# Retention attention and two dense layers on one core: the swapped copy of q's chunk 3 is made by VectorE instead of loaded

## The chip, the core and the metric

The kernel runs on one core of a Trainium2 chip. The core has TensorE (matrix multiplication into PSUM), VectorE, ScalarE and GpSimd (elementwise work), and SyncE, whose queue issues nearly all transfers between HBM and the on-chip SBUF. The metric is the device time of one execution in microseconds.

## The reference

Three stages stand behind one another, all in float32. Sizes: 4 batches, 8 heads, 576 positions, head size 64; 2304 tokens of width 512; inner widths 2048 and 1024.

```python
scores = scale * np.matmul(q, k.transpose(0, 1, 3, 2))
gamma = 1.0 - 2.0 ** (-5.0 - np.arange(H))
Dmat = np.where(rel >= 0, gamma[:, None, None] ** rel[None], 0.0)
x = np.matmul(scores * Dmat[None], v)                  # retention attention
...
h = x @ w_in
x = (h * np.clip(h + 3.0, 0.0, 6.0) / 6.0) @ w_out     # first dense stage
...
h = x @ w_in2
solu = h * softmax(h)
out = (layernorm(solu) * g_ln) @ w_out2                # second dense stage
```

## The kernel before, in words

Only the attention stage is touched. It works on 16 pairs of heads (pair 0 to 15; two heads of 64 rows fill the 128 partitions, `HEADS[0]` the lower half, `HEADS[1]` the upper). A pair's 576 positions are cut into four chunks of 128 and a rest of 64. Inside a chunk the scores are computed directly; what comes from earlier chunks goes through a running 64x64 state per head.

Per pair four tensors are loaded by SyncE: `rk` (k transposed), `rq` (q transposed), `rv` (v), `rn` (k in natural layout); `load_pair`, lines 415 to 425. The first three pairs, the early ones, go to tiles named `raw`. Loads run three pairs ahead. Behind pair 3's loads stands the first weight transfer, `wraw` (line 119), 512 KB.

The states of chunks 2 and 3 lie with the heads swapped between the halves of the partitions, so that `state[:, 2]` must meet a q of chunk 3 whose halves are swapped too. Before the change this swapped copy comes from HBM: the host appends it to `qt` as 128 further columns, and `rq[:, S:]` holds it. For pairs 3 to 15 it is a part of one transfer (352 KB instead of 288 KB), for the early pairs it is a fifth transfer of 64 KB (line 425).

The order per pair on TensorE is fixed by hand (`attention`, `mm_a`): scores `s`, last scores `z`, then `from_states` of the pair before (accumulates into `xp`, which has one buffer), the state updates `u` of this pair, `values` of the pair before (also into `xp`), and, from pair 4 on, six matmuls `h` of the first dense stage.

VectorE follows in program order. Per pair: L501 (`st4`, from `z`), L470 (state of chunk 0 copied from `u`), four multiply-adds L476 (the other states), and in between L527, `xa`: it takes the pair before out of `xp`. In every second pair come L147 and L148, the unpacking of a weight tile `wz`, and in the others L158 (its low part; for every third weight tile GpSimd does it) and L285 (`gf`, the activation of the dense stage). ScalarE scales v (L436), takes the scores out of PSUM (`st`, L455), rounds `xa` to `xb` (L260), unpacks weights (L139 `wz`, L144 `wt`, L153 `w`) and does L284 (`r`) and L290 (`g`). GpSimd masks the scores (L456), and computes the low parts of `xb` (L261, two pieces per pair that together have 576 columns), of some weights (L158) and of `g` (L291). A line 71 is a helper for the later stages.

What sets the order off TensorE is a planner inside the framework, which places instructions that are not pinned; `keep` pins one behind the last pinned one.

Of the kernel before, what the change touches and what calls it, by code (L numbers as in the profile page):

```python
# [18 lines left out]
B, H, S, D = 4, 8, 576, 64  # L19
# [55 lines left out]
def retention_hardswish_solu_kernel(ctx, tc, kt, qt, kn, vt, w1, w2i, w2o, gln, decay, place, out):  # L75


    nc = tc.nc
    ve, se, ge, te, sy = nc.vector, nc.scalar, nc.gpsimd, nc.tensor, nc.sync
# [309 lines left out]
    raws, vs, sts, sts4, states, us, xps = {}, {}, {}, {}, {}, {}, {}  # L389
    HEADS, ALL = [slice(0, 64), slice(64, 128)], slice(0, 128)  # L390
    CHUNKS = [slice(128 * c, min(128 * c + 128, S)) for c in range(NV)]
# [5 lines left out]
    keep = tc.keep_in_program_order  # L397

    def mm_a(*args, **kw):
        keep(nc.tensor.matmul(*args, **kw))  # L400

    def load_pair(pr):

        if pr >= NPAIR:
            return
        early = pr < EARLY
        if early:
            tag = "wi" if pr < 2 else "g"
            rk, rq, rn = [p0.tile([128, n], F32, tag=tag, bufs=FA, name=f"raw{pr}_{i}")
                          for i, n in enumerate((S, S + 128, 512))]  # L410
        else:
            rk = pa.tile([128, S], F32, tag="rk", bufs=3, name=f"rk{pr}")
            rq = pa.tile([128, S + 128], F32, tag="rq", bufs=4, name=f"rq{pr}")
            rn = pa.tile([128, 512], F32, tag="rn", bufs=3, name=f"rn{pr}")
        nc.sync.dma_start(out=rk, in_=kt[pr])
        n = S if early else S + 128
        nc.sync.dma_start(out=rq[:, :n], in_=qt[pr][:, :n])
        if early:
            rv = p0.tile([128, 9, D], F32, tag="g", bufs=FA, name=f"rv{pr}")
        else:  # L420
            rv = pa.tile([128, 9, D], F32, tag="rv", bufs=3, name=f"rv{pr}")
        nc.sync.dma_start(out=rv, in_=vt[pr])
        nc.sync.dma_start(out=rn, in_=kn[pr])
        if early:
            nc.sync.dma_start(out=rq[:, n:], in_=qt[pr][:, n:])
        raws[pr] = rk, rq, rn.rearrange("p (c d) -> p c d", d=128), rv

    def prep(pr):
# [32 lines left out]
    def chunk_states(pr):  # L461

        rn, v = raws[pr][2], vs[pr]
        up = ps_a.tile([128, 4, 64], F32, tag="u", bufs=1, name=f"u{pr}")
        state = states[pr] = pa.tile([128, 4, 64], F32, tag="state", bufs=2, name=f"state{pr}")
        for c in range(4):
            for h in range(2):
                o = HEADS[1 - h if c == 3 else h]
                mm_a(up[o, c], rn[:, c, HEADS[h]], v[:, 4 * h + c], start=(c == 0), stop=(c == 3))
        ve.tensor_copy(out=state[:, 0], in_=up[:, 0])  # L470
        for c, to, at in (
            (1, ((ALL, ALL),), H + pr % NP), (2, tuple(zip(HEADS, HEADS[::-1])), H + pr % NP),
            (3, ((ALL, ALL),), H + 2 * NP + pr % NP),
        ):
            for i, o in to:
                ve.scalar_tensor_tensor(  # L476
                    out=state[o, c], in0=state[i, c - 1], scalar=decay_sb[i, at:at + 1], in1=up[i, c],
                    op0=ALU.mult, op1=ALU.add,
                )

    def places():

# [50 lines left out]
    def attention():  # L533

        for pr in range(NPAIR + 1):
            if pr < NPAIR:
                scores(pr)
                last_scores(pr)
            if pr:
                from_states(pr - 1)  # L540
            if pr < NPAIR:
                idle_mm(N_IDLE.get(pr, 0))
                if pr == 0:
                    places()
            yield pr
            if pr < NPAIR:
                load_pair(pr + EARLY)
                chunk_states(pr)
                prep(pr + 1)
                if pr < NP:  # L550
                    widen(pr)
            yield pr
            if pr:
                values(pr - 1)
            yield pr
            if pr == 1:
                tc.keep_in_program_order(nc.sync.dma_start(out=gln_sb, in_=gln))
# [16 lines left out]
    for pr in range(EARLY):  # L574
        load_pair(pr)
# [3 lines left out]
    for h in range(2):  # L579
        ge.affine_select(  # L580
            out=mask4[HEADS[h]], in_=mask4[HEADS[h]], compare_op=ALU.is_ge, fill=0.0,
# [332 lines left out]
    ve, se, ge, te, sy = (Pinned(tc, e) for e in (ve, se, ge, te, sy))  # L914
# [145 lines left out]
```

## Time and profile before

| | |
|---|---|
| median of 3 runs | 650.05 us (649.01 to 650.99) |
| profiled execution | 651.0 us, of which the span from first to last instruction is 649.3 |
| TensorE busy | 641.0 us (99%) |
| VectorE, ScalarE, GpSimd busy | 333.5 (51%), 370.0 (57%), 325.8 us (50%) |
| transfers | 114.01 MB, mean 176 GB/s |
| attention stage | about the first 84 us of the span |

The shares say how much an engine works in all, not who is waited for. Attention takes an eighth of the span, and there all engines hand work to each other pair by pair; so it is read from the engines' timelines, where the time in square brackets is the idle time before an instruction and the name behind it what ended it.

### The profile page before, as it was taken

How to read it: one execution, taken by the hardware profiler on the slowest of the kernel's cores; microseconds unless marked ns; L12 is line 12 of the kernel's file. 1: busy time of each engine (PE TensorE's matmuls, PEld its weight loads, DVE VectorE, ACT ScalarE, POOL GpSimd, SP SyncE). 2: the span in 40 equal slices, each digit the busy share in tenths (PEclk: the TensorE clock that was granted, in tenths of full speed). 3: DMA queues.
4: the chain of work that ended last, by engine and by line, in shares of the span. 5: the costliest groups of instructions: out<-in, count | busy, mean ns of one | idle time of the engine just before them, and what ended most of it. 6: DMA issues, size and time to landing. Idle time of an engine off the chain costs nothing.

```text
span 649.3 us, 11131 instructions
## 1 busy us (share of the span) xinstructions
PE 641.0 (99%) x4178; PEld 533.4 (82%) x4178; DVE 333.5 (51%) x618; ACT 370.0 (57%) x653; POOL 325.8 (50%) x342
## 2 busy tenths in 40 slices
PE   8899999999999999999999999999999999999998
PEld 5777878888889888888888888889988888888887
DVE  2767635334104454143555446112588878878750
ACT  5788846556325665164356337215277768787582
POOL 4687844223222434045044014606379899999453
PEclk9999999999999999999999999999999999999999
DMA  8999517277015161557765645239795333534442
GB/s 307 371 380 365 208 33 260 97 260 258 33 41 191 63 194 59 169 195 292 257 218 161 240 158 167 97 121 369 256 229 145 81 98 99 130 81 98 74 104 68
DMA packets 80459, 114.01 MB, mean 176 GB/s; under 512 B 42642, under 2 KB 47890, under 8 KB 80404
## 3 DMA queue, kind: packets, MB, share of 16 engines
q1 hardware_dynamic: 80256, 113.27, 55.0%
q8 instruction: 33, 0.54, 0.4%
q14 instruction: 22, 0.18, 0.1%
q10 hardware_dynamic: 148, 0.02, 0.0%
HBM read 71.85 MB, written 31.98 MB: 160 GB/s over the span
## 4 chain that ended last, share of the span: by engine, by line
PE 95%; DMA 3%; ACT 1%; issue 0%; DVE 0%; SPq 0%; ACTq 0%
PE h L272 31%; PE x L297 20%; PE o L71 15%; PE h L71 13%; PE acc L297 8%; PE xp L400 3%; PE x L71 2%; PE s L400 2%; DMA wraw<-in_w_dram 1%; PE u L400 1%; DMA raw<-in_qt_dram 1%; DMA raw<-in_kn_dram 1%; DVE w L158 0%; PE z L400 0%; ACT st L455 0%
## 5 line engine op out<-in xcount | busy, mean ns | idle before, releaser
L291 POOL TENSOR_TENSOR g<-gf,g 128x512 fp32r<-128x512 f32 (+1 forms) x78 | 96.5, 1237 | 215.2 <-ACT g L290 205.1
L297 PE MATMUL x<-g,w 128*128 128x512 f32 x576 | 132.0, 389 | 0.0
L272 PE MATMUL h<-xb,w 128*128 128x512 f32 (+1 forms) x600 | 129.8, 360 | 0.1
L297 PEld LDWEIGHTS x<-g,w 128*128 128x128 f32 x576 | 108.1, 188 | 22.5
L272 PEld LDWEIGHTS h<-xb,w 128*128 128x128 f32 x600 | 98.5, 189 | 17.9 <-issue 1.9
L285 DVE SCALAR_TENSOR_TENSOR gf<-r,h 128x512 f32<-128x512 f32 (+1 forms) x80 | 50.5, 632 | 120.1 <-ACT r L284 105.0
L71 PE MATMUL o<-w,lt 128*128 128x512 f32 (+1 forms) x456 | 103.0, 378 | 0.0
L71 PEld LDWEIGHTS o<-w,lt 128*128 128x128 f32 x456 | 82.4, 188 | 16.3 <-POOL lt L71 0.4
L284 ACT ACTIVATE r<-h,half 128x512 f32<-128x512 f32 (+1 forms) x80 | 50.6, 635 | 64.4 <-PE h L272 64.4
L272 PE MATMUL h<-xB,w 128*128 128x512 f32 x360 | 82.4, 389 | 0.0
L272 PEld LDWEIGHTS h<-xB,w 128*128 128x128 f32 x360 | 67.6, 188 | 14.0
L290 ACT ACTIVATE g<-gf 128x512 fp32r<-128x512 f32 (+1 forms) x78 | 46.1, 591 | 44.0 <-DVE gf L285 38.6
L71 POOL TENSOR_TENSOR lt<-lT,lt 128x512 fp32r<-128x512 f32 x36 | 61.0, 1713 | 13.4 <-ACT lt L71 13.4
L297 PE MATMUL acc<-g,w 128*128 128x512 f32 (+1 forms) x264 | 61.9, 361 | 0.0
L71 ACT ACTIVATE e<-h,stat 128x1024 f32<-128x1024 f32 x36 | 41.3, 1148 | 34.9 <-DVE stat L71 34.8
L297 PEld LDWEIGHTS acc<-g,w 128*128 128x128 f32 x264 | 46.9, 188 | 8.8
L147 DVE TENSOR_SCALAR wz<-wz 128x512 int32<-128x512 int32 x44 | 29.5, 671 | 47.7 <-ACT wz L139 47.6
L71 PE MATMUL h<-w2t,xt 128*128 128x512 f32 x216 | 53.5, 389 | 0.0
L71 PEld LDWEIGHTS h<-w2t,xt 128*128 128x128 f32 x216 | 40.3, 188 | 8.2
L71 PE MATMUL h<-w2b,xt 128*128 128x512 f32 x162 | 39.8, 390 | 0.0
L139 ACT ACTIVATE wz<-wraw 128x512 f32<-128x512 f32 x44 | 29.2, 663 | 17.6 <-DMA wraw<-in_w_dram 8.9
L261 POOL TENSOR_TENSOR xb<-xa,xb 128x512 fp32r<-128x512 f32 (+7 forms) x32 | 28.3, 906 | 16.8 <-ACT xb L260 16.6
(114 smaller groups left out, 842.9 us busy)
## 6 DMA issues: line engine op xcount, KB each, us to landing
wraw<-in_w_dram SPq DMA_DIRECT2D x32, 512.0 KB, 5.0
xs<-xb SPq DMA_DIRECT2D x12, 512.0 KB, 7.7
xB<-xs SPq DMA_DIRECT2D x12, 512.0 KB, 6.3
rv<-in_vt_dram SPq DMA_DIRECT2D x16, 288.0 KB, 6.3
x2l<-x2s SPq DMA_DIRECT2D x18, 256.0 KB, 4.2
x2f<-x2o SPq DMA_DIRECT2D x18, 256.0 KB, 3.6
x2r<-x2f SPq DMA_DIRECT2D x9, 512.0 KB, 4.4
rq<-in_qt_dram SPq DMA_DIRECT2D x13, 352.0 KB, 6.8
```

Of the source, the lines that this page charges most:

```text
L71: return lambda *args, **kw: self.keep(op(*args, **kw))
L139: first = se.activation(out=z.bitcast(F32), in_=raw[:, :, 1].bitcast(F32), func=ACTF.Prelu, scale=2.0 ** -112, alpha=2.0 ** 32)
L147: ve.tensor_scalar(out=z, in0=z, scalar1=3, scalar2=None, op0=ALU.logical_shift_left)
L261: ge.tensor_tensor(out=x[:, 1, c], in0=src, in1=f32(x[:, 0, c]), op=ALU.subtract)
L272: mm = nc.tensor.matmul(hp, w1t[ff, 0][:, a, c], xb[t, p][:, b, :n], start=(p == 0 and i == 0), stop=(p == NP - 1 and i == 2),)
L284: se.activation(out=r, in_=hp, func=ACTF.Relu, scale=1.0 / 6.0, bias=half)
L285: ve.scalar_tensor_tensor(out=gf, in0=r, scalar=1.0, in1=hp, op0=ALU.min, op1=ALU.mult)
L290: se.activation(out=g[ff][:, 0], in_=gf, func=ACTF.Copy)
L291: ge.tensor_tensor(out=g[ff][:, 1], in0=gf, in1=f32(g[ff][:, 0]), op=ALU.subtract)
L297: te.matmul(acc, w1t[ff, 1][:, a, c], g[:, b], start=(first and i == 0), stop=(last and i == 2))
L400: keep(nc.tensor.matmul(*args, **kw))
```

## The change

The host no longer appends the swapped chunk; `load_pair` loads the 576 columns of q for every pair, in one transfer each. In `chunk_states` VectorE copies the two halves of chunk 3 crosswise into `rq[:, S:]` (two copies of 64 partitions x 128 columns), ahead of the states. These copies, the state copy and the multiply-adds are now pinned.

```diff
--- before.py
+++ after.py
@@ -413,16 +413,13 @@
             rq = pa.tile([128, S + 128], F32, tag="rq", bufs=4, name=f"rq{pr}")
             rn = pa.tile([128, 512], F32, tag="rn", bufs=3, name=f"rn{pr}")
         nc.sync.dma_start(out=rk, in_=kt[pr])
-        n = S if early else S + 128
-        nc.sync.dma_start(out=rq[:, :n], in_=qt[pr][:, :n])
+        nc.sync.dma_start(out=rq[:, :S], in_=qt[pr])
         if early:
             rv = p0.tile([128, 9, D], F32, tag="g", bufs=FA, name=f"rv{pr}")
         else:
             rv = pa.tile([128, 9, D], F32, tag="rv", bufs=3, name=f"rv{pr}")
         nc.sync.dma_start(out=rv, in_=vt[pr])
         nc.sync.dma_start(out=rn, in_=kn[pr])
-        if early:
-            nc.sync.dma_start(out=rq[:, n:], in_=qt[pr][:, n:])
         raws[pr] = rk, rq, rn.rearrange("p (c d) -> p c d", d=128), rv
 
     def prep(pr):
@@ -467,16 +464,19 @@
             for h in range(2):
                 o = HEADS[1 - h if c == 3 else h]
                 mm_a(up[o, c], rn[:, c, HEADS[h]], v[:, 4 * h + c], start=(c == 0), stop=(c == 3))
-        ve.tensor_copy(out=state[:, 0], in_=up[:, 0])
+        rq = raws[pr][1]
+        for h in range(2):
+            keep(ve.tensor_copy(out=rq[HEADS[1 - h], S:], in_=rq[HEADS[h], CHUNKS[3]]))
+        keep(ve.tensor_copy(out=state[:, 0], in_=up[:, 0]))
         for c, to, at in (
             (1, ((ALL, ALL),), H + pr % NP), (2, tuple(zip(HEADS, HEADS[::-1])), H + pr % NP),
             (3, ((ALL, ALL),), H + 2 * NP + pr % NP),
         ):
             for i, o in to:
-                ve.scalar_tensor_tensor(
+                keep(ve.scalar_tensor_tensor(
                     out=state[o, c], in0=state[i, c - 1], scalar=decay_sb[i, at:at + 1], in1=up[i, c],
                     op0=ALU.mult, op1=ALU.add,
-                )
+                ))
 
     def places():
 
@@ -1016,7 +1016,6 @@
     kt, qt = (np.array(a.transpose(0, 2, 1).reshape(NPAIR, 2 * D, S)) for a in (k, q))
     for a in (kt, qt):
         a[:, :, 512:] = np.roll(a[:, :, 512:], D, axis=1)
-    qt = np.concatenate([qt, np.roll(qt[:, :, 384:512], D, axis=1)], axis=2)
     kn = k[:, :512].reshape(NPAIR, 2, 4, 128, D).transpose(0, 3, 2, 1, 4).reshape(NPAIR, 128, 512)
     vt = np.empty((NPAIR, 128, 9, D), np.float32)
     vt[:, :, :8] = v[:, :512].reshape(NPAIR, 2, 4, 128, D).transpose(0, 3, 1, 2, 4).reshape(NPAIR, 128, 8, D)
```

TensorE's, ScalarE's and GpSimd's instructions keep their order. VectorE's and SyncE's change in attention alone. Three places follow; the number behind a name belongs to the buffer and differs between the two kernels.

VectorE in the states of pair 4, where a weight tile's L158 stands; before:

```order
L476 SCALAR_TENSOR_TENSOR state_471<-state_471,decay_sb,u_470 128x64
L501 TENSOR_TENSOR st_535<-z_534,mask_116 128x64
L158 TENSOR_TENSOR w_0_0_507<-wz,w_0_0_507 128x512
L470 COPY state_559<-u_558 128x64
L476 SCALAR_TENSOR_TENSOR state_559<-state_559,decay_sb,u_558 128x64
L476 SCALAR_TENSOR_TENSOR state_559<-state_559,decay_sb,u_558 64x64 x2
L527 TENSOR_TENSOR xa_593<-xp_539,tab_sb_115 128x576
```

L158 stands between L501 and the state copy. The same stretch of VectorE in the changed kernel:

```order
L501 TENSOR_TENSOR st_540<-z_539,mask_116 128x64
L469 COPY rq_283<-rq_283 64x128
L158 TENSOR_TENSOR w_0_0_512<-wz,w_0_0_512 128x512
L469 COPY rq_283<-rq_283 64x128
L470 COPY state_564<-u_563 128x64
L476 SCALAR_TENSOR_TENSOR state_564<-state_564,decay_sb,u_563 128x64
L476 SCALAR_TENSOR_TENSOR state_564<-state_564,decay_sb,u_563 64x64 x2
L527 TENSOR_TENSOR xa_600<-xp_544,tab_sb_115 128x576
```

The low part of the weights, L158, was ahead of the state copy and is now between the two copies of q's halves.

VectorE around pair 13, from the weights' L147 on (`state_1433` before, `state_1456` after, is pair 13's); before:

```order
L147 TENSOR_SCALAR wz<-wz 128x512
L148 ISA wz<-wz,wt 128x1024
L501 TENSOR_TENSOR st_1417<-z_1416,mask_116 128x64
L470 COPY state_1433<-u_1432 128x64
L476 SCALAR_TENSOR_TENSOR state_1433<-state_1433,decay_sb,u_1432 128x64
L476 SCALAR_TENSOR_TENSOR state_1433<-state_1433,decay_sb,u_1432 64x64 x2
L527 TENSOR_TENSOR xa_1459<-xp_1421,tab_sb_112 128x576
```

The state copy follows L501 directly. The same stretch of VectorE in the changed kernel:

```order
L147 TENSOR_SCALAR wz<-wz 128x512
L148 ISA wz<-wz,wt 128x1024
L501 TENSOR_TENSOR st_1440<-z_1439,mask_116 128x64
L469 COPY rq_1156<-rq_1156 64x128 x2
L470 COPY state_1456<-u_1455 128x64
L476 SCALAR_TENSOR_TENSOR state_1456<-state_1456,decay_sb,u_1455 128x64
L476 SCALAR_TENSOR_TENSOR state_1456<-state_1456,decay_sb,u_1455 64x64 x2
L527 TENSOR_TENSOR xa_1484<-xp_1444,tab_sb_112 128x576
```

Two copies are added between L501 and the state copy; the rest stands as it did, with `xa` of pair 12 behind the states. The same two copies stand at this place in every pair.

SyncE's transfers of pair 2 and pair 3, up to the first weight transfer; before:

```order
L415 DMA raw_0_152<-in_kt_dram 128x576
L417 DMA raw_1_153<-in_qt_dram 128x576
L422 DMA rv_157<-in_vt_dram 128x576
L423 DMA raw_2_154<-in_kn_dram 128x512
L425 DMA raw_1_153<-in_qt_dram 128x128
L415 DMA rk_209<-in_kt_dram 128x576
L417 DMA rq_210<-in_qt_dram 128x704
L422 DMA rv_214<-in_vt_dram 128x576
L423 DMA rn_211<-in_kn_dram 128x512
L119 DMA wraw<-in_w_dram 128x1024
```

Ten transfers, of which the fifth and a part of the seventh carry the swapped chunk. The same stretch of SyncE's queue in the changed kernel:

```order
L415 DMA raw_0_150<-in_kt_dram 128x576
L416 DMA raw_1_151<-in_qt_dram 128x576
L421 DMA rv_155<-in_vt_dram 128x576
L422 DMA raw_2_152<-in_kn_dram 128x512
L415 DMA rk_206<-in_kt_dram 128x576
L416 DMA rq_207<-in_qt_dram 128x576
L421 DMA rv_211<-in_vt_dram 128x576
L422 DMA rn_208<-in_kn_dram 128x512
L119 DMA wraw<-in_w_dram 128x1024
```

The fifth transfer of the early pairs is gone and pair 3's q has 576 columns instead of 704.

## Rows read from the trace of the kernel before

**Rows 1.** DMA view, 0 to 90 us: GB/s in 40 slices of 2.25 us

```profile
GB/s 46 305 327 394 333 359 371 377 394 374 380 371 356 362 322 374 392 395 400 397 362 349 331 404 395 366 277 396 413 372 313 364 144 7 16 220 7 0 195 38
```

**Rows 2.** Stretches: us, busy us of each engine, granted clock, DMA share, GB/s

```profile
0.00:26.40 26.40, 21.72 (x420) 15.35 (x420) 10.52 (x34) 16.10 (x37) 13.97 (x35) 1.00 0.94 335
...
84.00:649.30 565.30, 562.14 (x2703) 472.78 (x2692) 283.10 (x479) 305.27 (x507) 266.51 (x251) 1.00 0.51 155
```

**Rows 3.** Chain of waits, 0 to 140 us: start us, us, what

```profile
12.80 7.50 DMA wraw<-in_w_dram
```

**Rows 4.** Timeline, TensorE: start us, us, engine, line, operation, count, [idle before]

```profile
22.76 1.48 PE L400 MATMUL s<-rq,rk 64*64 64x128 f32 x29 [1.57 <-ACT st L455]
...
24.33 0.27 PE L400 MATMUL xp<-st,v 64*64 64x64 f32 x2
...
48.59 0.22 PE L400 MATMUL xp<-st,v 64*64 64x64 f32 x2
...
79.27 4.47 PE L272 MATMUL h<-xb,w 128*128 128x512 f32 x18
```

**Rows 5.** Timeline, VectorE, 20 to 84 us

```profile
22.35 0.21 DVE L470 COPY state<-u 128x64 f32<-128x64 f32 x1
...
23.52 0.76 DVE L527 TENSOR_TENSOR xa<-xp,tab_sb 128x576 f32<-128x576 f32 x1
...
30.75 0.23 DVE L470 COPY state<-u 128x64 f32<-128x64 f32 x1 [0.19 <-PE u L400]
...
45.30 0.23 DVE L470 COPY state<-u 128x64 f32<-128x64 f32 x1
...
46.49 0.76 DVE L527 TENSOR_TENSOR xa<-xp,tab_sb 128x576 f32<-128x576 f32 x1
...
68.84 0.22 DVE L501 TENSOR_TENSOR st<-z,mask 128x64 f32<-128x64 f32 x1
69.19 0.23 DVE L470 COPY state<-u 128x64 f32<-128x64 f32 x1
...
70.37 0.76 DVE L527 TENSOR_TENSOR xa<-xp,tab_sb 128x576 f32<-128x576 f32 x1
```

**Rows 6.** Timeline, ScalarE, 38 to 84 us

```profile
48.91 0.78 ACT L260 ACTIVATE xb<-xa 128x448 fp32r<-128x448 f32 x2
...
68.09 0.77 ACT L260 ACTIVATE xb<-xa 128x384 fp32r<-128x384 f32 x2
...
71.16 0.78 ACT L260 ACTIVATE xb<-xa 128x320 fp32r<-128x320 f32 x2
```

**Rows 7.** Timeline, GpSimd, 20 to 84 us

```profile
22.16 1.54 POOL L261 TENSOR_TENSOR xb<-xa,xb 128x512 fp32r<-128x512 f32 x2 [3.52 <-ACT xb L260]
...
30.06 1.79 POOL L261 TENSOR_TENSOR xb<-xa,xb 128x512 fp32r<-128x512 f32 x2 [1.48 <-ACT xb L260]
...
44.77 1.29 POOL L158 TENSOR_TENSOR w<-wz,w 128x512 fp32r<-128x512 f32 x1
46.01 1.30 POOL L291 TENSOR_TENSOR g<-gf,g 128x512 fp32r<-128x512 f32 x1
...
68.69 1.65 POOL L261 TENSOR_TENSOR xb<-xa,xb 128x384 fp32r<-128x384 f32 x2 [1.13 <-ACT xb L260]
```

**Rows 8.** Tile wz (count: ns min/median/max), then GpSimd and VectorE from their timelines

```profile
L147 DVE TENSOR_SCALAR wz<-wz x37: 419/429/1498, 84.4 to 401.5; 128x512 int32<-128x512 int32 x37
...
96.19 1.29 POOL L291 TENSOR_TENSOR g<-gf,g 128x512 fp32r<-128x512 f32 x1 [6.61 <-ACT g L290]
...
96.70 1.06 DVE L147 TENSOR_SCALAR wz<-wz 128x512 int32<-128x512 int32 x1 [1.25 <-ACT wz L139]
...
240.86 1.65 POOL L291 TENSOR_TENSOR g<-gf,g 128x512 fp32r<-128x512 f32 x1 [4.95 <-ACT g L290]
242.47 1.75 POOL L158 TENSOR_TENSOR w<-wz,w 128x512 fp32r<-128x512 f32 x1
...
241.46 1.60 DVE L158 TENSOR_TENSOR w<-wz,w 128x512 fp32r<-128x512 f32 x1
```

## The prediction

> **What bounds the kernel now.** I read the page's shares first, then the stretches, the chain of waits, and last the timelines of the engines through attention. The granted clock is 1.00 in the stretches, so it plays no part [rows 2]. After 84 us TensorE is busy 562.14 of 565.30 us [rows 2]: what comes later there has at most 3.2 us of idle time in which to be made good, and the change touches none of it. What counts is attention, the first 84 us.
>
> Attention has two parts. Until some 26 us the transfers set the pace: TensorE is busy 21.72 of 26.40 us, and the chain runs through a weight transfer that is issued at 12.80 and takes 7.50 us, so to 20.30 [rows 2, 3]. ScalarE stands in line behind it with the states that free the score banks, and TensorE waits 1.57 us before 22.76 for them [rows 4]. From there TensorE runs pair after pair almost without a gap, some 4.8 us a pair (VectorE's state copies of pairs 5 and 13, at 30.75 and 69.19, stand 38.44 apart) [rows 5].
>
> VectorE and ScalarE look half idle in the shares, and they are not free. In pair 13 VectorE's L501 starts at 68.84 and the state copy at 69.19; three multiply-adds follow, and xa from 70.37 to 71.13; ScalarE's xb, which reads it, starts at 71.16 [rows 5, 6]. From there w, r, gf, g, st, wz, wt and xb of the other pair follow each other, and VectorE takes up L148 and L501 again. This circle takes two pairs and keeps step with TensorE, with 0.2 us to spare before the state copy (0.35 from L501's start, of which some 0.15 is L501 itself). TensorE's own slack is larger: in pair 8 xa ends at 47.25 and TensorE overwrites its bank from 48.59, 1.3 us later [rows 4, 5].
>
> **What goes: 16 pieces of 64 KB.** Ahead of the weight transfer four go (three transfers of line 425, and 64 of pair 3's 352 KB). From 2.25 to 20.25 us the slices read 305 to 394 GB/s, mean 357 [rows 1], so 65,536 bytes take 0.18 us, four 0.73. The transfer lands that much earlier, and so does TensorE's 22.76. The three issues that go from SP's queue were ahead of the same transfer and fall into this. The other twelve pieces lie in the part where TensorE never waits for a load: nothing.
>
> **What comes: 32 copies on VectorE**, two per pair, 64x128 fp32 from SBUF to SBUF, between L501 and the state copy. The rows hold no such copy. The nearest are the state copy (0.23 us, 64 elements, from PSUM) and L147 (fp32-sized, SBUF to SBUF, 512 elements: 0.42 at its shortest) [rows 5, 8]. Alone I put a copy at 0.07 (a quarter of what L147 takes below once it may run) to 0.23 us, and take 0.15, the middle.
>
> The larger question is GpSimd. L147 takes 0.419 to 1.498 us [rows 8], and the long ones are those that meet a GpSimd instruction: at 96.70 it is issued while GpSimd works from 96.19 to 97.48, and ends at 97.76, 0.28 after it. It does not run slower beside it, it waits for the end. And the two take turns: GpSimd's g, at 240.86, lasts 1.65 us and ends at 242.51; VectorE's L158, issued at 241.46, ends 0.55 later, at 243.06; the GpSimd instruction that stands behind, recorded at 242.47, takes 1.75 instead of 1.29, as it waits for VectorE in its turn.
>
> The Trainium skill (SBUF — State Buffer, section "Who interferes with whom") states it as a rule that speaks against this change: a copy in VectorE's two-port mode and a GpSimd instruction shut each other out for a whole instruction, and the one issued first goes first. By that rule the sum below holds; were a 64-partition copy outside it, the second rival would. The trace agrees for L147 (0.42 alone, 1.06 behind GpSimd); no row shows such a copy. The skill's table of VectorE costs (VectorE: DVE Perf Modes, section on the TRN2 errata) gives 58 cycles and half a cycle per element, an estimate of 0.13 us a copy; by it the sum would end some 0.3 us lower.
>
> So what does GpSimd do where the copies now stand? In the odd pairs ScalarE's xb (68.09, directly behind wt) hands the first of two L261 pieces to GpSimd at 68.69, while VectorE is in L148; L501 follows at 68.84, and a copy can be issued from about 69.0 [rows 5 to 7]. Both sides start from the same wt, so GpSimd stays ahead even when everything is late. The first copy waits for the first piece; then GpSimd's second piece, which has been waiting, goes ahead of the second copy. The state copy starts after both pieces and both copies. In pair 13 L261 ends at 70.34, the state copy stood at 69.19: 1.15 later, in pair 5 31.85 against 30.75, 1.10; these are the first and the last of five pairs (5, 7, 9, 11, 13). With two copies of 0.15 that makes 1.42 each. Nothing hides it: xa is queued behind on VectorE, xb behind xa on ScalarE, and the circle returns to VectorE that much later.
>
> **The sum.** Lateness of the circle against the trace:
> - pair 3: L261 ends at 23.70, plus 0.30 makes 24.00 against 22.35, 1.65, less the 0.73 of the start: 0.9. TensorE feels it at once: xa ends at 24.28 and TensorE's 24.33 follows it [rows 4, 5, 7].
> - pair 4: the order puts L158 between its copies; the second one waits for it and for a small piece of L261: some 0.4, the two copies and a handover.
> - pairs 5, 7, 9, 11, 13: 5 x 1.42 = 7.1.
> - pairs 8 and 14, where GpSimd also has the weights' L158 (44.77 and, behind it, g at 46.01 to 47.31): the copies wait for both, so the state copy moves from 45.30 to 47.6, 2.3 later; xa ends at 49.55. ScalarE's xb for it stood at 48.91: 0.64 more for the circle. TensorE's 48.59 waits for it too: 0.96 [rows 4 to 7].
> - pairs 6, 10, 12: GpSimd is idle there; 0.3 to 0.5 on VectorE lies under TensorE's slack of 1.3 and off the circle. Pairs 0 to 2 wait for TensorE anyway: nothing. Pair 15 lies under the h matmuls of 4.47 us from 79.27 [rows 4].
>
> Up to pair 14 the circle is late by 0.9 + 0.4 + 7.1 + 0.64 = 9.0; in pair 14 TensorE waits another 0.96, so it is late by 10.0 when attention ends, and keeps it, since it has no idle time later. The profiled run took 651.0 us (span 649.3, 1.7 around it): 661.0. It stands 0.95 above the median of 650.05, so the forecast is 660.0. With copies of 0.07 or 0.23, 14 of them in this sum, it moves by 1.1 either way; if TensorE's slack of 1.3 were kept to the end, 658.7; if the bank waits behind attention add up, 662. Own range 656.5 to 664.
>
> **Rivals.**
> - *Only the first copy waits.* The second follows before GpSimd's second piece. L261's first piece has 384 of 576 columns, some 1.1 of the 1.65 us, so pair 13 waits to 69.8: 0.6 + 0.3 = 0.9, five of them 4.5, with 0.5 from pair 3 and 0.4 from pair 4; pair 8 waits to 46.06, within the slack: 5.4, so 655.5. For it: the copies stand side by side in VectorE's queue. Against: at 241.46 the waiting GpSimd went before VectorE's next instruction. 0.17.
> - *The copies do not wait for GpSimd at all*, as the state copy does not. An odd pair then costs two copies (0.46 at most) less 0.2, so 0.3; five make 1.3, pairs 3 and 4 some 0.9, less 0.73: 1.5, of which TensorE's slack takes most: 650.5. For it: only half the partitions, other shapes than in the rows. Against: L147 and its length. 0.13.
> - *The other side: the start decides.* If copies are free and the thinner queue of loads clears not only the 0.73 but all of the wait of 1.57 before 22.76 and some of the rest of the start (26.40 less 21.72 is 4.7 us of idle time), TensorE gains 2 us: 648. It decides once VectorE is done with pair 3's states before 22.35 + 0.73. Against: GpSimd works from 22.16 to 23.70 just there. 0.06.
> - That the change is not carried out is excluded by the order of the instructions, which shows 32 copies and three transfers fewer.
>
> **Chances.** The forecast 0.64, the rivals 0.17, 0.13, 0.06. About 0.3%, 2 us, is what a measurement of this kernel can tell from no change. Slower by more: the forecast, the first rival and a little of the second, 0.82; within: most of the second and some of the third, 0.13; faster: 0.05. The range reaches down through the first rival, 652.5, and up to 665.
>
> **What would show it.** VectorE's line 469 with two classes: some 0.2 us alone (pairs 6, 10, 12) and 0.5 to 1.2 us beside GpSimd, each ending shortly after a GpSimd instruction; in the odd pairs L261's second piece between the two copies. TensorE with waits of 1 us and more per two pairs in front of xp or s, put down to xa or st, and the h matmuls of 79.27 some 10 us later. The first weight transfer 0.7 us earlier. It is wrong if the copies are short everywhere (650.5), or if the circle has slack that I do not see, such as a wait of ScalarE for TensorE that swallows the lateness; then TensorE's pairs stay some 4.8 us apart.

## The result, and the profile after

The changed kernel takes **657.83 us** (median of 4 runs, 657.39 to 658.13) against 650.06 (649.01 to 650.99): 1.0134 times as long, 95% interval 1.0122 to 1.0147. It is slower by 7.8 us; 660.0 were predicted, 656.5 to 664 as the likeliest case's own range.

Its profiled execution took 657.54 us, span 655.7. The stretches (us, busy us of each engine, granted clock, DMA share, GB/s), to be held against [rows 2]:

```profile
0.00:26.40 26.40, 23.11 (x424) 16.23 (x426) 14.70 (x46) 17.52 (x40) 15.57 (x37) 1.00 0.97 351
26.40:90.00 63.60, 58.55 (x1071) 46.32 (x1069) 50.82 (x126) 47.06 (x106) 44.06 (x55) 1.00 0.74 254
90.00:655.70 565.70, 562.02 (x2690) 472.47 (x2686) 282.70 (x480) 306.41 (x508) 267.10 (x252) 1.00 0.51 155
```

The same view of the kernel before, for the part of attention behind the start:

```profile
26.40:84.00 57.60, 57.10 (x1068) 45.26 (x1070) 39.87 (x106) 48.64 (x111) 45.30 (x58) 1.00 0.85 306
```

Behind 90 us TensorE idles 3.7 us, hardly more than the 3.2 of before. Between 26.4 and 90 us it now idles 5.1 of 63.60 us, where it idled 0.5 of 57.60. What was lost was lost in attention. VectorE's timeline there (start, us, line, operation, count, [idle before]), answering to [rows 5]:

```profile
19.97 1.34 DVE L469 COPY rq<-rq 64x128 f32<-64x128 f32 x2
...
46.24 2.04 DVE L469 COPY rq<-rq 64x128 f32<-64x128 f32 x2
48.20 0.21 DVE L470 COPY state<-u 128x64 f32<-128x64 f32 x1
...
68.48 0.46 DVE L469 COPY rq<-rq 64x128 f32<-64x128 f32 x2
...
72.81 0.22 DVE L501 TENSOR_TENSOR st<-z,mask 128x64 f32<-128x64 f32 x1
73.05 1.34 DVE L469 COPY rq<-rq 64x128 f32<-64x128 f32 x2
74.31 0.21 DVE L470 COPY state<-u 128x64 f32<-128x64 f32 x1
...
75.48 0.76 DVE L527 TENSOR_TENSOR xa<-xp,tab_sb 128x576 f32<-128x576 f32 x1
```

And GpSimd's timeline, answering to [rows 7]:

```profile
45.67 1.28 POOL L158 TENSOR_TENSOR w<-wz,w 128x512 fp32r<-128x512 f32 x1
46.91 1.29 POOL L291 TENSOR_TENSOR g<-gf,g 128x512 fp32r<-128x512 f32 x1
...
69.06 1.27 POOL L291 TENSOR_TENSOR g<-gf,g 128x512 fp32r<-128x512 f32 x1 [0.89 <-ACT g L290]
...
72.66 1.65 POOL L261 TENSOR_TENSOR xb<-xa,xb 128x384 fp32r<-128x384 f32 x2 [1.15 <-ACT xb L260]
```

The two copies of pair 12 (68.48) meet an idle GpSimd and take 0.46 us together. Those of pair 13 (73.05) meet the two pieces of L261, which end at 74.31, and the state copy starts at 74.31. One by one these four are:

```profile
73.05 0.78 DVE L469 COPY rq<-rq 64x128 f32<-64x128 f32 x1
73.85 0.54 DVE L469 COPY rq<-rq 64x128 f32<-64x128 f32 x1
72.66 1.09 POOL L261 TENSOR_TENSOR xb<-xa,xb 128x384 fp32r<-128x384 f32 x1 [1.15 <-ACT xb L260]
73.71 0.60 POOL L261 TENSOR_TENSOR xb<-xa,xb 128x192 fp32r<-128x192 f32 x1
```

The first copy ends at 73.83, 0.08 behind the first piece (73.75), and the second at 74.39, 0.08 behind the second (74.31). Those of pair 8 (46.24) meet the weight's L158 and, behind it, g, which ends at 48.20; the state copy starts at 48.20. Of the 32 copies 15 last 0.22 to 0.27 us, the others 0.41 to 1.26.

TensorE's timeline shows who waits for it:

```profile
20.28 1.94 PE L400 MATMUL s<-rq,rk 64*64 64x128 f32 x32 [0.52 <-ACT st L452]
...
50.18 0.27 PE L400 MATMUL xp<-st,v 64*64 64x64 f32 x2 [0.83 <-DVE xa L527]
...
82.88 0.27 PE L400 MATMUL xp<-st,v 64*64 64x64 f32 x2 [0.86 <-DVE xa L527]
...
94.55 2.96 PE L297 MATMUL acc<-g,w 128*128 128x512 f32 x12 [0.51 <-DVE xa L527]
```

TensorE's waits for xa in the first 95 us are, in the kernel before and then in the changed one (us in total, times, longest):

```profile
PE xp L400 <- DVE xa L527: 0.2, 1, 0.2
PE xp L400 <- DVE xa L527: 4.0, 7, 0.9
```

The first row of the timeline above starts 2.48 us earlier than its partner at 22.76, though, where 0.73 had been predicted; the first weight transfer landed at 17.74 instead of 20.30:

```profile
10.34 7.40 DMA wraw<-in_w_dram
```

This is the chain of waits, against [rows 3]. Two questions stood open: whether the turns with GpSimd are the whole price, and what the start is worth.

### The profile page after: what moved, and what is told of

It is laid out like the page before. It is cut to its first block, busy times and chain, and to the rows that moved or that the text cites. A ratio compares the mean times of both kernels' runs of the same rounds, so it can differ in the third digit from the quotient of the medians.

```text
span 655.7 us, 11157 instructions
## 1 busy us (share of the span) xinstructions
PE 643.7 (98%) x4177; PEld 535.0 (82%) x4178; DVE 348.2 (53%) x650; ACT 371.0 (57%) x653; POOL 326.7 (50%) x342
## 4 chain that ended last, share of the span: by engine, by line
PE 88%; DMA 4%; POOL 3%; DVE 2%; ACT 1%; issue 1%; SPq 0%; ACTq 0%; DVEq 0%; POOLq 0%
PE h L272 28%; PE x L297 20%; PE o L71 15%; PE h L71 13%; PE acc L297 8%; DMA wraw<-in_w_dram 3%; PE x L71 2%; POOL xb L261 1%; POOL st L453 1%; DVE xa L527 1%; PE xp L400 1%; DMA raw<-in_kt_dram 1%; ACT xb L260 1%; PE s L400 1%; PE u L400 1%
## 5 line engine op out<-in xcount | busy, mean ns | idle before, releaser
L147 DVE TENSOR_SCALAR wz<-wz 128x512 int32<-128x512 int32 x44 | 29.7, 675 | 44.4 <-ACT wz L139 44.3
L261 POOL TENSOR_TENSOR xb<-xa,xb 128x512 fp32r<-128x512 f32 (+7 forms) x32 | 29.4, 940 | 24.1 <-ACT xb L260 24.1
```

What stands on the lines that cost most here:

```text
L147: ve.tensor_scalar(out=z, in0=z, scalar1=3, scalar2=None, op0=ALU.logical_shift_left)
L261: ge.tensor_tensor(out=x[:, 1, c], in0=src, in1=f32(x[:, 0, c]), op=ALU.subtract)
```

## The experiments

All ratios are to the kernel before on the same chip, with a 95% interval. The median of the kernel before is 650.06 us in the result above and 648.72 to 649.14 in the experiments, so times of different experiments are compared through the ratios.

### The copies alone

The loads of the kernel before, and the copies on top:

```diff
+        for h in range(2):
+            keep(ve.tensor_copy(out=rq[HEADS[1 - h], S:], in_=rq[HEADS[h], CHUNKS[3]]))
```

> The loads of the kernel before and the copies of the changed one (which write the same numbers over what was loaded). It shows the price of the copies alone. Theory (copies cost some 8 to 10 us over their waits, the loads' gain is separate): the changed kernel's 657.8 and the start's 2 to 2.5 on it, 659.5 to 660.5 us. Rival (the load's gain is 0.73): 658.6 us. Second rival (what slows attention is that loads are missing, not the copies): 650 us.

Measured: 658.66 against 649.14 us, 1.0146 (1.0133 to 1.016), so 9.5 us. The copies carry the whole loss. Against 1.0134 for the changed kernel the missing loads are worth 0.8 us, with an uncertainty (some 1.2) larger than the number.

### Half as long

```diff
-keep(ve.tensor_copy(out=rq[HEADS[1 - h], S:], in_=rq[HEADS[h], CHUNKS[3]]))
+keep(ve.tensor_copy(out=rq[HEADS[1 - h], S:S + 64], in_=rq[HEADS[h], 384:448]))
```

> As the kernel with loads and copies, but each copy moves the first 64 of the 128 columns (the rest stays as loaded): 32 copies of half the length. Theory (a copy costs the end of the GpSimd instruction that it meets, whatever its length): 1.0 to 1.015 times the kernel before, close to the 1.0146 of whole copies: 1.013 (1.011 to 1.0145), and a copy that meets GpSimd idle takes some 0.15 us instead of 0.22. Rival (elements are paid for, by VectorE's own time or by the share of a port): half of the surplus, 1.007.

Measured: 1.0147 (1.0133 to 1.0161), a hair above the range expected and the same as with whole copies. The row of this tile on VectorE (count: ns min/median/max, first and last start):

```profile
L472 DVE COPY rq<-rq x26: 189/517/1258, 20.9 to 86.2; 64x64 f32<-64x64 f32 x26
```

Half the elements save 32 ns where a copy is alone (189 against 221 with whole copies) and nothing where it waits (1258 against 1257). Elements aren't what is paid for.

### Half as many

```diff
-        for h in range(2):
+        for h in range(1):
             keep(ve.tensor_copy(out=rq[HEADS[1 - h], S:], in_=rq[HEADS[h], CHUNKS[3]]))
```

> As the kernel with loads and copies, but one copy for a pair instead of two. Theory (a price for each turn with GpSimd): in odd pairs the state copy starts at the end of the first piece of the subtraction, 0.56 us earlier than with two (0.6 instead of 1.15 late), and in pairs 8 and 14, which meet 1.3 us instructions, 1.2 us earlier: 5 x 0.56 + 2 x 1.2 = 5.2 of the 9.5 us go, ratio to the kernel before 1.0066 (1.005 to 1.009). Rival (the first copy alone waits, the second rides behind it for nothing): 1.0135 or more.

Measured: 1.0084 (1.0068 to 1.0099), 5.5 us: one copy less saves 4.0 of the 9.5, somewhat less than the 5.2 worked out. The rival, that the first copy alone waits, would have left all of it. From L501's start to the state copy's, pair 8 takes 1.07 us instead of 2.21, and the odd pairs from 5 to 13 take 1.07 to 1.34 instead of 1.51 to 1.52. There is a price for each turn.

### The same place and length, another form

```diff
-            keep(ve.tensor_copy(out=rq[HEADS[1 - h], S:], in_=rq[HEADS[h], CHUNKS[3]]))
+            keep(ve.tensor_reduce(
+                out=rq[HEADS[1 - h], S:], in_=rq[HEADS[h], CHUNKS[3]].unsqueeze(2), op=ALU.add, axis=AX.X,
+            ))
```

> The copies stay ahead of the state copy, in another form of the same length: a sum over an axis of one element, 64x128 each. Theory (it is the turn with GpSimd that costs, and this form takes no turn): each lasts about 0.2 to 0.25 us beside GpSimd's subtraction, the pair's two 0.45, of which 0.2 fits into the slack of the odd pairs: six such pairs by 0.25 are 1.5 over the 648.0 of no cost, so about 649.5 us (648.5 to 651.5). Rival (VectorE's own time for two more instructions, or what their pins do to its order, is the price): 657.8 us as the changed kernel, since there are as many instructions in the same places. Second rival (this form waits for GpSimd as well): 0.5 to 0.8 us each in odd pairs, 657 to 659 us.

Measured: 650.97 us, 1.0021 (1.001 to 1.0031). That is 1.4 us over the kernel before by this ratio and 1.8 by the medians, where the changed kernel loses 7.8. VectorE around the same pair 13:

```profile
67.73 0.69 DVE L148 CUSTOM_DVE_ANT_0 wz<-wz,wt 128x1024 uint16<-128x1024 uint16 x1 [0.15 <-ACT wt L144]
68.34 0.22 DVE L503 TENSOR_TENSOR st<-z,mask 128x64 f32<-128x64 f32 x1
68.59 0.57 DVE L469 TENSOR_REDUCE rq<-rq 64x128 f32<-64x128 f32 x2
69.08 0.21 DVE L472 COPY state<-u 128x64 f32<-128x64 f32 x1
```

and GpSimd beside it, in the same kernel:

```profile
68.19 1.66 POOL L261 TENSOR_TENSOR xb<-xa,xb 128x384 fp32r<-128x384 f32 x2 [1.17 <-ACT xb L260]
```

L261 works from 68.19 to 69.85, and both sums run in the middle of it in 0.57 us. All 26 on this tile last 279 to 284 ns. As many instructions in the same places, each a little longer than a lone copy, cost about a fifth: most of the price is the wait and not VectorE's time. By the Trainium skill (SBUF — State Buffer, "Who interferes with whom") a sum over an axis never contends with GpSimd on this chip, while a copy in two-port mode does. The trace agrees on both: 0.28 us for each sum beside L261, against 0.78 and 0.54 for the two copies at the same place.

### The loads alone, and the pins alone

Without the extra loads and without copies:

```diff
-        for h in range(2):
-            keep(ve.tensor_copy(out=rq[HEADS[1 - h], S:], in_=rq[HEADS[h], CHUNKS[3]]))
...
-            (1, state[:, 0], rq[:, CHUNKS[1]]), (3, state[:, 2], rq[:, S:]),
+            (1, state[:, 0], rq[:, CHUNKS[1]]), (3, state[:, 2], rq[:, CHUNKS[3]]),
```

> Neither the extra load nor the copies; the matmuls of chunk 3 read the chunk unswapped (left out: the swap of its halves). It shows the price of the loads alone. Theory (the start won 2 to 2.5 us because the weight transfer landed at 17.7 where it had landed at 20.3): 648.0 us (647.3 to 648.8). Rival (four pieces of 64 KB are worth 0.73 us at the rate of the slices, and the rest of the earlier landing was chance of one run): 649.3 us (648.9 to 649.6).

Measured: 649.12 against 649.14 us, 1.0002 (0.9992 to 1.0012). My theory's 2 to 2.5 us fell. The rival's 649.3 was reckoned from 650.05; against this chip's 649.14 even its 0.73 isn't seen.

The kernel before with the pins, which moved no instruction on any engine:

> The kernel before with only the pins on the state copy and the multiply-adds; on every engine its instructions stand in the same order as before, so its profile is also a second look at the kernel before. Theory (pins cost nothing, and the late scores of pair 3 in the profile of before, at 22.76 us, were one execution's chance in the first loads): within 0.1 % of before, and TensorE begins pair 3's scores near 20.3 to 21.0 us. Rival (the loads of the extra chunk made that start late every time): the scores begin at 22.3 to 22.9 us again. Second rival (pins cost): over 1 us slower than before.

Measured: 1.0005 (0.9996 to 1.0013); the pins cost nothing. Its profile (span 647.6) is a second look at the kernel before. SyncE's and TensorE's timelines there:

```profile
11.43 0.33 SPq L119 DMA_DIRECT2D wraw<-in_w_dram  x1
```

```profile
21.07 1.83 PE L400 MATMUL s<-rq,rk 64*64 64x128 f32 x31 [1.50 <-ACT st L455]
...
77.59 4.47 PE L272 MATMUL h<-xb,w 128*128 128x512 f32 x18
```

The weight transfer is issued at 11.43 and takes 7.2 us, so it lands at 18.6; the scores begin at 21.07, and the 18 h matmuls 1.68 us earlier than in [rows 4]. The execution of before that I had read was a late one: by 1.4 to 1.7 us from pair 2 to its end. In the four experiments that have all the extra loads the transfer lands at 18.5 to 18.7; in the eight profiles that lack those ahead of it, the changed kernel's 17.74 among them, at 17.6 to 18.1. The middles are 0.8 apart: 0.73 was the right size.

Finally the lighter start alone: extra chunk not loaded for pairs 0 to 3, and loaded for the rest.

```diff
-        n = S if early else S + 128
+        n = S if pr <= EARLY else S + 128
...
-        if early:
-            nc.sync.dma_start(out=rq[:, n:], in_=qt[pr][:, n:])
...
+        for h in range(2 if pr <= EARLY else 0):
+            keep(ve.tensor_reduce(...))
```

> The extra piece is left out of the loads of pairs 0 to 3 alone, whose swap is done by the summing form ahead of the state copy; pairs 4 to 15 as in the kernel before. It shows what the lighter start is worth when nothing is paid for it later. Theory (the start's gain in the changed kernel's profile was chance of one execution of the kernel before; four pieces of 64 KB are worth 0 to 0.7 us and TensorE gives them back in the circle): 0.9995 (0.9985 to 1.001). Rival (2.5 us as in the profiles): 0.996 to 0.997.

Measured: 648.63 against 648.93 us, 0.9997 (0.9988 to 1.0007). The landing of the weights comes earlier, the end does not, to within 0.7 us. Where it goes isn't settled.

### Where else the copies can stand

Behind the states, where VectorE idles before L147 or L158:

```diff
-            keep(ve.tensor_copy(out=rq[HEADS[1 - h], S:], in_=rq[HEADS[h], CHUNKS[3]]))
-        keep(ve.tensor_copy(out=state[:, 0], in_=up[:, 0]))
+        ve.tensor_copy(out=state[:, 0], in_=up[:, 0])
...
+            keep(ve.tensor_copy(out=rq[HEADS[1 - h], S:], in_=rq[HEADS[h], CHUNKS[3]]))
```

> The same 32 copies in the same form, moved from ahead of the state copy to behind the last multiply-add of the pair, where VectorE idles; loads as in the changed kernel. Theory (the copies wait for GpSimd's subtractions ahead of the state copy, and this wait stretches the circle VectorE - ScalarE - GpSimd): the wait leaves the circle and the earlier start stays, so about 648.0 us (647.0 to 649.5), faster than both kernels; the copies may still last 0.2 to 0.9 us each, and it costs nothing. Rival (fewer loads or the pins are what slows attention, or the copies cost wherever they stand on VectorE): 655 to 658 us.

Measured: 651.15 us, 1.0031 (1.0019 to 1.0043), faster than the changed kernel by 1.0% and still slower than before, where the theory had it faster. TensorE in pairs 0 and 1:

```profile
10.55 0.80 PE L400 MATMUL xp<-raw,state 64*64 64x128 f32 x12 [0.46 <-DVE raw L479]
...
15.56 0.27 PE L400 MATMUL xp<-st,v 64*64 64x64 f32 x2 [0.81 <-DVE xa L527]
```

In the first pairs the copies stand ahead of what TensorE waits for. So the sums took the first four pairs, ahead of the states, and the copies the rest, behind them:

```diff
+        for h in range(2 if pr <= EARLY else 0):
+            keep(ve.tensor_reduce(...))
...
+        for h in range(2 if pr > EARLY else 0):
+            keep(ve.tensor_copy(out=rq[HEADS[1 - h], S:], in_=rq[HEADS[h], CHUNKS[3]]))
```

> No extra load; the first four pairs swap by the summing form ahead of the state copy, the others by copies behind the last multiply-add. Theory (what the copies behind the states cost was in the first pairs, where xa and the matmuls of chunk 3 stood behind them, and what the summing form cost was in the later ones): both costs go, ratio 1.000 to the kernel before (0.999 to 1.0015), as with neither load nor copy, and some 1.3 % faster than the changed kernel. Rival (every placement costs some 1.5 us, by the time that it takes from VectorE): 1.002 to 1.003.

Measured: 650.71 us, 1.0034 (1.0022 to 1.0047). The theory's 1.000 fell, and the number is just above what the rival gave. VectorE in pair 4 shows a reason other than the rival's:

```profile
27.01 0.48 DVE L483 COPY rq<-rq 64x128 f32<-64x128 f32 x2
27.52 0.43 DVE L147 TENSOR_SCALAR wz<-wz 128x512 int32<-128x512 int32 x1
28.09 1.55 DVE L148 CUSTOM_DVE_ANT_0 wz<-wz,wt 128x1024 uint16<-128x1024 uint16 x1
29.56 0.21 DVE L505 TENSOR_TENSOR st<-z,mask 128x64 f32<-128x64 f32 x1
```

with GpSimd beside it:

```profile
27.58 2.23 POOL L261 TENSOR_TENSOR xb<-xa,xb 128x512 fp32r<-128x512 f32 x2 [1.27 <-ACT xb L260]
```

The copies wait for nothing, but L147 and L148 come behind them, and L148, otherwise 0.69 us, runs into L261's two pieces (27.58 to 29.81) and lasts 1.55. In the other pairs L148 still lasts 0.69, so this is 0.86 of some 2 us; the rest isn't accounted for pair by pair. So I put nothing ahead of L147: the odd iterations, which have none, swap two pairs at once, the own by copies, the next by sums:

```diff
+        if pr >= 5 and pr % 2:
+            swap(pr, False)
+            if pr + 1 < NPAIR:
+                swap(pr + 1, True)
```

> No extra load; nothing more ahead of L147 and L148: the first five pairs swap by the summing form ahead of the state copy, and from pair 5 on the odd iterations, which have no L147, swap their own pair by copies and the next pair by the summing form behind the last multiply-add, in the 1.1 us in which VectorE waits for the weight's words. Theory (what placement behind the states cost was that the copies pushed L147 and L148 0.5 us later, into GpSimd's subtraction: L148 lasted 1.55 us instead of 0.69 in pair 4): the surplus goes, ratio 1.000 to the kernel before (0.999 to 1.0015); L148 lasts 0.69 us in all pairs. Rival (the time on VectorE, 0.45 to 0.56 us a pair, costs wherever it stands): 1.0025 to 1.004 as in the last run.

Measured: 651.35 us, 1.0034 (1.0022 to 1.0046). L148 lasts 0.69 throughout, as expected, and the surplus stays, so L148 alone was not what cost it. VectorE's copies again:

```profile
L471 DVE TENSOR_REDUCE rq<-rq x14: 279/280/282, 20.4 to 73.2; 64x128 f32<-64x128 f32 x14
L472 DVE COPY rq<-rq x12: 444/644/1203, 31.1 to 81.5; 64x128 f32<-64x128 f32 x12
...
  PE xp L400: 1.4, 3
```

The last row is who waited for them: TensorE's chunk 3, 1.4 us in three places. No copy is short any more; GpSimd selects `st` and then subtracts in just this stretch, as in pair 9 (two copies, and GpSimd beside them):

```profile
51.25 1.51 DVE L472 COPY rq<-rq 64x128 f32<-64x128 f32 x2
50.40 1.22 POOL L453 TENSOR_SCALAR_AFFINE_SELECT st<-st 128x512 f32<-128x512 f32 x2
51.67 1.56 POOL L261 TENSOR_TENSOR xb<-xa,xb 128x384 fp32r<-128x384 f32 x2
```

The last kernel changes only these copies to sums:

```diff
-            swap(pr, False)
+            swap(pr, True)
```

> As the last kernel but one, with the two halves of the own pair in the odd iterations in the summing form too: no swap takes the form of a copy any more, and all stand behind the states from pair 5 on. Theory (what was left there was again the turn with GpSimd: the copies met its selection of st and its next subtraction, lasted 0.44 to 1.20 us and held the matmuls of chunk 3 up): every swap lasts 0.28 us, 1.12 for four beside 1.1 us of idle time, and the ratio to the kernel before falls from 1.0034 to 1.000 (0.999 to 1.0015). Rival (the time on VectorE costs wherever it stands): 1.003 to 1.004 again.

Measured: **648.62 against 648.84 us, 0.9999 (0.9985 to 1.0012)**. All 26 last 279 to 282 ns, and nobody waits for them. VectorE in this kernel:

```profile
49.68 1.20 DVE L471 TENSOR_REDUCE rq<-rq 64x128 f32<-64x128 f32 x4
50.91 0.74 DVE L158 TENSOR_TENSOR w<-wz,w 128x512 fp32r<-128x512 f32 x1
```

The four sums fill the gap ahead of L158 with 1.20 us of work, and the 2 us are gone. It makes the swap without its loads at no cost, 1.3% faster than the changed kernel, and no faster than the kernel before: with neither loads nor copies there was nothing to be had.

## Why the prediction was right, and where its sizes were off

The second look at the kernel before (span 647.6) is the better measure for single steps, since its start is not late.

- **The start, 0.73.** The transfer lands some 0.8 earlier. That this is kept to the end was wrong or is too small to see: 0.0 and -0.2 us with 0.7 either way in the two runs that have it alone. The third rival (the start decides, 648) is refuted by the same two runs.
- **A copy takes 0.07 to 0.23 alone, 0.15 taken.** It takes 0.22, so the upper end. With it the sum would have grown by 1 us. The copies did not add even the 0.15: one that waits ends 0.08 behind GpSimd's instruction, whatever it takes alone, and in pair 13 the state copy starts at L261's end (74.31) and not 0.3 behind it.
- **Copies wait for GpSimd, both of them.** Right, by the rows above, and shown by the sums, which run beside L261. The first rival (only the first copy waits, 655.5) is refuted by the run with one copy. The second (no wait) describes the kernel with the sums. Its 650.5 was 0.45 above the kernel before, and the sums cost 1.4 by their ratio, so its price was too low.
- **The lateness of the circle, 9.0 up to pair 14.** VectorE's state copy of pair 15, in the second look and in the changed kernel:

```profile
76.84 0.23 DVE L470 COPY state<-u 128x64 f32<-128x64 f32 x1
86.00 0.21 DVE L470 COPY state<-u 128x64 f32<-128x64 f32 x1
```

  It is 9.16 late. That this meets 9.0 is in part luck, since the terms behind it are off both ways. Up to pair 4 the sum had 1.3, and the state copy of pair 4 is 0.46 late. From there to pair 13 it had 7.74, and 6.35 are lost. For pairs 14 and 15 it had nothing in the circle (0.96 on TensorE), and 2.35 are lost. An odd pair was put at 1.42 and an even one beside it (6, 10, 12) at nothing; from state copy to state copy the even ones lose 0.35 to 0.5 as well and the odd ones 0.5 to 0.9, so two pairs lose 1.0 to 1.3 together. The state copies of pairs 8 and 9 lose 2.0 and 0.04, where 0.64 and 1.42 stood: 2.05 against 2.06.
- **TensorE 10.0 late at the end: the step that failed.** The sum made TensorE as late as the circle from pair 3 on, added 0.96 in pair 14, and took nothing off for its slack of 1.3. TensorE where it overwrites xa's bank in pair 14, in the second look (the changed kernel's row is the one at 82.88 above), and the 18 h matmuls of the changed kernel:

```profile
75.44 0.22 PE L400 MATMUL xp<-st,v 64*64 64x64 f32 x2
...
84.97 4.46 PE L272 MATMUL h<-xb,w 128*128 128x512 f32 x18
```

  xa itself is 8.71 late in pair 14 (82.07 against 73.36), and TensorE behind it 7.44 (82.88 against 75.44). The difference is 1.27: in the second look TensorE comes 1.32 behind the end of xa there, in the changed kernel 0.05. So it follows the circle at the distance of the slack that [rows 4, 5] show, which is used up once. The h matmuls, which were to come some 10 us later, come 7.4 later (84.97 against 77.59). TensorE then waits 0.51 more at 94.55 for xa's bank, and the kernel ends 8.1 late (spans 655.7 and 647.6). The text gave this branch a price, 658.7 with the slack kept; 657.83 was measured. What is left between them, 0.9 us, isn't split up further.

## What to carry to other kernels

A copy between SBUF tiles on VectorE, as small as those here (64 partitions, 64 or 128 columns, float32), is cheap by its length and dear by its place: beside a busy GpSimd it waits for the end of the instruction that it meets, once for each copy, whichever of the two lengths it has. Look for GpSimd's intervals at the exact place before adding one, and also at the place of the shared instructions that it would push back; or take a form that does not wait, as the sum over an axis of one element here (0.28 us everywhere, against 0.22 to 1.26). Its place still counts: ahead of the state copy in every pair the sums cost 1.4 us; behind the states from pair 5 on they cost nothing that could be measured. And take a second profile of the same instructions before an early start is credited to an edit: here 1.7 us between two executions would have passed for a gain.

## What the runs showed that was not expected

A copy of 64 columns takes 189 ns and one of 128 takes 220: twice the columns add some 31 ns, so most of the time doesn't depend on the length. The prediction's estimate of 0.13 us in all took the fixed 58 cycles of a table in the Trainium skill (VectorE: DVE Perf Modes, section on the TRN2 errata). The same section says that this row comes out too low, and that the measured fixed term is about 150 cycles; with it the estimate is 0.22 us. The trace agrees, with 0.220.

The unpacking L148 waits for GpSimd as well (1.55 instead of 0.69 us in pair 4). And GpSimd's selection L453 holds copies up just as its subtractions do: the first of the two at 51.25 above lasts 0.44 us and ends behind it.
